# Top-32 attention with a channel mix: groups of four tiles over passes of 256 rows, inverse row sums turned by halves

## The chip, the cores and the metric

The kernel runs on one core of a Trainium2 chip. The metric is device time in microseconds (us), from the first to the last instruction as the runtime measures it; the number compared is the median of several executions. Inside the core five engines work side by side and meet through semaphores: TensorE (PE, matrix products; its weight loads are listed as PEld), VectorE (DVE), ScalarE (ACT), GpSimd (POOL) and SyncE (SP, which here only issues the copies between the chip's main memory and the core).

## The reference

Inputs are q, k, v of shape (8 batches, 8 heads, 576 rows, 64) and the parameters of a channel mix of width 512 with 1024 hidden units.

```python
scores = scale * q @ k.T                       # per batch and head, 576 x 576
kth    = 32nd largest of each row
attn   = exp(where(scores >= kth, scores, -1e9) - rowmax)
attn   = attn / (attn.sum(-1) + 1e-9)
x      = (attn @ v), heads side by side        # (8, 576, 512)
x_prev = x moved down by one row, per batch
xk, xr = mu * x + (1 - mu) * x_prev            # with mu_k and mu_r
k      = relu(xk @ w_k);  v = (k * k) @ w_v
out    = sigmoid(xr @ w_r) * v
```

## The kernel before, in words

**Attention tiles.** Heads go in pairs (HP = 4 pairs). A *tile* is 128 partitions of scores against all 576 keys: in a unit with w > 1 it is 128 query rows of one head (two tiles, j = 0 and 1, for the two heads of the pair); in a unit with w = 1 it is 64 rows of both heads, one head in each half of the partitions. There are 288 tiles. Rows of one batch are cut by PARTS into *visits*, and these into *units* of w = 4, 2 or 1 tiles, since 576 is not a multiple of 256: over four batches there are 14 units for each pair of heads, six of w = 4, four of w = 2, four of w = 1; over the eight batches and four pairs that is 48, 32 and 32 units, 112 in all. A visit loads its queries, its half of the pair's v into one of two buffers, and, on the first visit of a batch and pair, the keys into one of four homes.

**Slots.** The program is written out by hand, slot by slot: slot n starts tile n and carries earlier tiles one stage further, in the sequence ORDER. `score` (L205; L210, or L214 for w = 1) puts the tile into PSUM, ACT copies it out (`keep`, L219), DVE picks candidates over six slots, POOL multiplies (L260), DVE masks (L271). Five slots after the score `turn_tile` (L283) transposes the tile in ten pieces of 64 rows. When the tile is the last of its unit, `inverse` (ACT, L291), `inverse2` (DVE, L295) and `spread` (POOL, L300) make the inverse row sums; one slot later `turn_inverse` (L307, one 128 x 128 transpose for two tiles) and `weigh` (L333, the product with v, 10 matmuls for 128 rows) follow, ACT takes both results out of PSUM (L312 or L316, L339 or L341), and `place` (POOL, L345) multiplies them into x of the batch, in the slot seven after the last score.

**The mix.** The channel mix goes in 18 chunks of 256 rows, each in 40 *pieces* of six or three matmuls (L388 to L390): 8 gate pieces (tile pz), 16 hidden pieces (ph), 16 value pieces (pv). Each chunk runs gates, the second half of the values of the chunk before, hidden, then its own first half of the values. A chunk can begin when all heads have placed its 256 rows; then differences (L358), shares (L363), sums (L368), and a split into a high and a low part (ACT L383, L384) come ahead of its gates. L388 is executed once for each gate or value piece and twice for each hidden piece, 56 times in a chunk.

**The planner.** `Lanes` holds a budget for each engine. PE gets 3.45 a slot, and keeps at most 3.75. A score takes 0.70 from it, a transposed tile 0.45, a unit that is weighed 0.27 w + 0.30 and 0.13 for each transpose of its inverse sums; a piece of the mix takes 0.72, and is issued while at least 0.74 of that is left, at most four a slot:

```python
if done == most or L.free["pe"] < cost * SHARE:
    return done
L.use("pe", cost)
```

In the last 36 slots a piece counts 0.56. After the last tile, VectorE takes over the mix's work of GpSimd.

Of the kernel before, what the change touches and what calls it, by code (L numbers as in the profile page):

```python
# [29 lines left out]
WHOLE = [(0, 4), (256, 4), (512, 1)]  # L30
PARTS = [[(0, 4)], [(256, 4)], [(512, 1)]], [[(0, 1), (64, 2)], [(192, 4)], [(448, 2)]], \
    [[(0, 2)], [(128, 4)], [(384, 2), (512, 1)]], [[(0, 1)], [(64, 4)], [(320, 4)]]
# [15 lines left out]
def topk_attention_channel_mix(ctx: ExitStack, tc: tile.TileContext, q, k, v, mu_k, mu_r, w_k, w_v, w_r, out):  # L48
# [19 lines left out]
    least = consts.tile([128, 3 * B], F32, name="least")  # L68
# [11 lines left out]
    def open_pools(stack, g, sfx):  # L80
# [10 lines left out]
        g.sums = scored[:, :, HS:HS + 128], scored[:, 0, HS + 128:HS + 192]  # L91
# [79 lines left out]

    def load_keys(g, P, batch, hp):
        P.K = g.one.tile([128, 2, HS], F32, name="K", tag=f"K{P.home}")
        for i in range(2):
            nc.sync.dma_start(P.K[i * 64:(i + 1) * 64], heads(k, batch, hp)[:, :, i * HS:(i + 1) * HS].rearrange("h d s -> d h s"))

    def load_queries(g, P, batch, hp, c0, c1):
        P.c0 = c0
        P.qs = g.three.tile([128, 2, c1 - c0], F32, name="qs")
        for i in range(2):  # L180
            nc.sync.dma_start(P.qs[i * 64:(i + 1) * 64], heads(q, batch, hp)[:, :, c0:c1].rearrange("h d s -> d h s"))

    def load_v(g, P, batch, hp):
        P.v = g.two.tile([128, 2, NKC, D], F32, name="v_in")
        P.vr = vr_hf[P.n % 2]
        h = heads(v, batch, hp)
        for j in range(2):
            nc.sync.dma_start(P.v[:, j], h[j, :MAIN].rearrange("(c p) d -> p c d", p=128))
        nc.sync.dma_start(P.vr[64:], h[:, MAIN:].rearrange("h p d -> p h d"))

    def units_of(shape):

        units, tiles = [], []
        for row, w in shape:
            U = Env()
            U.row, U.w = row, w
            units.append(U)
            for k in range(w):
                T = Env()
                T.U, T.k, T.t, T.u, T.j, T.row = U, k, len(tiles), k // 2, k % 2, row + k // 2 * 128  # L200
                T.last = k == w - 1
                tiles.append(T)
        return units, tiles

    def scores(g, P, T):  # L205
        hs = [slice(e * 64, (e + 1) * 64) for e in range(2)]
        x = T.row - P.c0
        if T.U.w > 1:
            for e, h in enumerate(hs):
                nc.tensor.matmul(g.ps[:, e], lhsT=P.qs[h, T.j, x:x + 128], rhs=P.K[h, T.j], start=True, stop=True)  # L210
        else:
            for j in range(2):
                for e, h in enumerate(hs):
                    nc.tensor.matmul(g.ps[hs[j], e], lhsT=P.qs[h, j, x:x + 64], rhs=P.K[h, j], start=True, stop=True)  # L214
        return g.ps
# [57 lines left out]
    def turn_tile(g, T, L):  # L273
        U, j, u = T.U, T.j, T.u
        if T.k == 0:
            U.et = {}
        et = U.et[u, j] = (g.two if j else g.three).tile([128, NKC + 1, 128], F32, name=f"et{j}")
# [11 lines left out]
    def inverse(g, U):  # L289
        rs = U.rs[:, :U.w]  # L290
        nc.scalar.activation(rs, rs, AF.Copy, bias=1e-9)  # L291

    def inverse2(U):
        rs = U.rs[:, :U.w]
        nc.vector.reciprocal(rs, rs)  # L295

    def spread(g, U):
        w, d = U.w, 64 if U.w > 1 else 128
        U.rb = g.one.tile([128, w, d], F32, name="rb")
        nc.gpsimd.tensor_scalar(U.rb, U.rs[:, :w, None].to_broadcast([128, w, d]), 1.0, 1.0, op0=OP.mult, op1=OP.mult)  # L300

    def turn_inverse(g, U, L):
        rb = U.rb.rearrange("p h d -> p (h d)")
        pr = g.pt[:, :, 384:]
        n = (U.w + 1) // 2
        for u in range(n):
            nc.tensor.transpose(pr[:, u], rb[:, u * 128:(u + 1) * 128], ident)  # L307

        def out_():
            U.ri = g.two.tile([128, 256], F32, name="ri")  # L310
            if U.w > 1:
                nc.scalar.activation(U.ri[:, :n * 128].rearrange("p (u q) -> p u q", u=n), pr[:, :n], AF.Copy)  # L312
            else:
                for j in range(2):
                    h = slice(j * 64, (j + 1) * 64)
                    nc.scalar.activation(U.ri[h, :64], pr[h, 0, h], AF.Copy)  # L316
        L.at(0, "late", out_)

    def weigh(g, U, u):
        P = U.P  # L320
        if u == 0:
            U.pa = g.sums[U.w == 1]
        hs = [slice(j * 64, (j + 1) * 64) for j in range(2)]
        if U.w > 1:
            pa = U.pa[:, u]
            ms = [[U.et[u, j][:, c, :] for j in range(2)] for c in range(NKC + 1)]
        else:
            pa = U.pa
            ms = [[U.et[0, 0][:, c, h] for h in hs] for c in range(NKC + 1)]
        for c in range(NKC + 1):  # L330
            for j in range(2):
                lhsT = P.v[:, j, c, :] if c < NKC else P.vr[:, j]
                nc.tensor.matmul(pa[hs[j]], lhsT=lhsT, rhs=ms[c][j], start=(c == 0), stop=(c == NKC))  # L333

    def take_sums(g, U):
        n = U.w // 2
        U.sum = g.two.tile([128, 256], F32, name="sum")
        if n:
            nc.scalar.activation(U.sum[:, :n * 128].rearrange("p (u q) -> p u q", u=n), U.pa[:, :n], AF.Copy)  # L339
        else:  # L340
            nc.scalar.activation(U.sum[:, :64], U.pa, AF.Copy)  # L341

    def place(U):
        n = U.w * 64
        nc.gpsimd.tensor_mul(U.xT[:, U.P.hp, 1 + U.row:1 + U.row + n], U.sum[:, :n], U.ri[:, :n])  # L345

    def begin(g, C, which, i, L):

        X, h0, n, pieces = Env(), 2 * i, C.n, C.pieces
        parts, o = [], 0  # L350
# [259 lines left out]
    def prep(g, P, batch, hp, c0, c1):  # L610
        load_keys(g, P, batch, hp)
        load_queries(g, P, batch, hp, c0, c1)
        load_v(g, P, batch, hp)

# [5 lines left out]
    def pipeline(g):  # L620
# [3 lines left out]
        visits = []  # L624
        for b in range(B):
            for k, shape in enumerate(PARTS[b % 4]):
                visits += [(b, hp, shape) for hp in (range(HP) if k % 2 == 0 else reversed(range(HP)))]
        starts = [0]
        for *_, shape in visits:
            starts.append(starts[-1] + sum(w for _, w in shape))  # L630
        where = [p for p in range(len(visits)) for _ in range(starts[p], starts[p + 1])]
        homes, held = {}, [(-1, None)] * KEYS
        for p, (b, hp, _) in enumerate(visits):
            home = next((h for h, (_, of) in enumerate(held) if of == (b, hp)), None)
            own, free = home is None, 0
            if own:
# [80 lines left out]
        def coming(n):  # L717

            for p in range(1, len(visits)):
                t = n - starts[p]  # L720
                if -8 <= t <= 6:
                    yield Ps[p] if p in Ps else new_pair(p), t
# [258 lines left out]
```

## Time and profile before

| | us |
|---|---|
| median of 3 runs | 1162.88 (1161.68 to 1163.26) |
| the profiled execution | 1162.55 |
| its span, first to last instruction | 1160.7 |
| PE busy | 1094.9 (94%) |
| DVE busy | 1073.9 (93%) |
| ACT busy | 991.4 (85%) |
| POOL busy | 968.3 (83%) |
| mean granted TensorE clock | 0.990 of full speed |

The median is 0.33 us above the profiled execution, which is 1.85 us above its own span. Busy time is a union over the stretch: matmuls are pipelined and their ends are modelled, so a PE that shows no gap can still hold short waits. Times in views are microseconds from the start of the span.

### The profile page before, as it was taken

To read this page: it belongs to the slowest core of one execution; us is meant where nothing else is said; L and a number is where in the kernel's file an instruction comes from. 1 tells how busy PE (TensorE), PEld (TensorE's weight loads), DVE (VectorE), ACT (ScalarE), POOL (GpSimd) and SP (SyncE) were. 2 spreads that over 40 slices of the span, in tenths; PEclk is the share of its full clock that TensorE was granted. 3 is DMA by queue.
4 is the path that set the end of the run, shared out by engine and by line. 5 is a ranking of instruction groups with operands and counts; after the bars stand their busy time and mean duration, and the time that the engine had idled before them with its cause. 6 is when DMAs were issued, how large, how long until landed. Compare 5 with 4: busy or idle time off the path is not lost.

```text
span 1160.7 us, 32775 instructions
## 1 busy us (share of the span) xinstructions
PE 1094.9 (94%) x10625; PEld 854.2 (74%) x10625; DVE 1073.9 (93%) x6009; ACT 991.4 (85%) x2121; POOL 968.3 (83%) x1069
## 2 busy tenths in 40 slices
PE   5777999999999999999999999999999999999998
PEld 2444776768787877787878777787878777878787
DVE  6999999999999999999999999999999999989742
ACT  5889999988898899989898989998989899879631
POOL 5898997998989798989898988898989898979800
PEclk9889999999999999999999999999999999999999
DMA  7434133113331233112211132212331223111100
GB/s 193 124 111 112 30 91 92 49 45 78 77 79 45 64 74 96 49 50 69 70 49 50 29 104 68 69 45 75 80 79 45 62 73 85 44 49 40 30 10 30
DMA packets 161363, 78.77 MB, mean 68 GB/s; under 512 B 125344, under 2 KB 154016, under 8 KB 161184
## 3 DMA queue, kind: packets, MB, share of 16 engines
q1 hardware_dynamic: 161184, 76.59, 25.1%
q8 instruction: 87, 1.43, 0.5%
q14 instruction: 92, 0.75, 0.2%
HBM read 67.11 MB, written 9.44 MB: 66 GB/s over the span
## 4 chain that ended last, share of the span: by engine, by line
PE 51%; POOL 18%; DVE 16%; ACT 12%; issue 2%; DMA 1%; SPq 0%; ACTq 0%; POOLq 0%; DVEq 0%
PE ps L333 10%; PE ps L210 7%; POOL sg L260 6%; PE pt L283 4%; DVE cand L243 4%; PE ph L388 3%; PE pv L388 3%; DVE E L271 3%; PE pv L390 3%; PE ph L389 3%; PE ph L390 3%; DVE seen L843 3%; PE pv L389 3%; PE pz L388 3%; ACT sc L219 3%
## 5 line engine op out<-in xcount | busy, mean ns | idle before, releaser
L243 DVE MAX8 cand<-sc 128x8 f32<-128x82 f32 (+1 forms) x2016 | 467.2, 232 | 10.5 <-ACT sc L219 10.4
L260 POOL TENSOR_TENSOR sg<-sc,sg 128x576 f32<-128x576 f32 x288 | 411.7, 1431 | 48.7 <-ACT sg L257 48.5
L219 ACT ACTIVATE sc<-ps 128x576 f32<-128x576 f32 x288 | 188.0, 653 | 99.6 <-PE ps L210 85.8
L271 DVE SCALAR_TENSOR_TENSOR E<-sc,seen,se 128x576 f32<-128x576 f32 x288 | 232.9, 809 | 0.7 <-DVE cand L243 0.3
L257 ACT ACTIVATE sg<-sc,seen 128x576 f32<-128x576 f32 x288 | 225.7, 784 | 4.4 <-DVE seen L843 3.4
L268 ACT ACTIVATE se<-sc,seen 128x576 f32<-128x576 f32 x288 | 215.7, 749 | 10.4 <-DVE E L271 10.1
L843 DVE MAX8 seen<-sg 128x8 f32<-128x576 f32 x288 | 216.5, 752 | 4.1 <-POOL sg L260 3.7
L210 PE MATMUL ps<-K,qs 64*128 64x288 f32 x1024 | 198.7, 464 | 11.6 <-ACT sc L219 6.3
L286 ACT ACTIVATE et<-pt 128x640 f32<-128x640 f32 x288 | 204.3, 710 | 6.0 <-PE pt L283 4.0
L283 PEld LDWEIGHTS pt<-ident,E 64*128 64x128 f32 x2880 | 132.9, 139 | 75.2 <-ACT sg L257 17.5
L246 DVE MAX8 seen<-cand 128x8 f32<-128x56 f32 x864 | 177.4, 205 | 0.1
L388 PE MATMUL ph<-xh,wk 128*128 128x256 f32 x576 | 172.2, 299 | 0.0
L333 PE MATMUL ps<-et,v_in 128*64 128x128 f32 (+1 forms) x2560 | 162.0, 269 | 8.4 <-ACT sc L219 7.2
L389 PE MATMUL ph<-xl,wk 128*128 128x256 f32 x576 | 162.2, 282 | 0.0
L390 PE MATMUL ph<-xh,wk 128*128 128x256 f32 x576 | 162.0, 281 | 0.0
L333 PEld LDWEIGHTS ps<-et,v_in 128*64 128x64 f32 x2560 | 131.4, 138 | 39.6 <-ACT sc L219 13.1
L283 PE MATMUL pt<-ident,E 64*128 64x64 f32 x2880 | 140.3, 224 | 15.3 <-DVE E L271 9.0
L210 PEld LDWEIGHTS ps<-K,qs 64*128 64x128 f32 x1024 | 79.5, 189 | 74.0 <-issue 24.7
L388 PE MATMUL pv<-wv,hh 128*128 128x512 f32 x288 | 123.7, 429 | 0.0
L390 PE MATMUL pv<-wv,hl 128*128 128x512 f32 x288 | 114.3, 397 | 8.7 <-POOL hl L409 8.7
L249 DVE MATCH_REPLACE8 cand<-seen,cand 128x56 f32<-128x56 f32 x576 | 115.4, 200 | 0.0
L389 PE MATMUL pv<-wv,hh 128*128 128x512 f32 x288 | 113.5, 394 | 0.0
(103 smaller groups left out, 2234.5 us busy)
## 6 DMA issues: line engine op xcount, KB each, us to landing
v_in<-in_v SPq DMA_DIRECT2D x192, 128.0 KB, 2.6
qs<-in_q SPq DMA_DIRECT2D x96, 128.0 KB, 2.9
K<-in_k SPq DMA_DIRECT2D x64, 144.0 KB, 3.0
out<-eb SPq DMA_DIRECT2D x36, 256.0 KB, 2.5
vr_in<-in_v SPq DMA_DIRECT2D x96, 32.0 KB, 2.5
hh<-in_moe_w_v SPq DMA_DIRECT2D x6, 512.0 KB, 4.1
qs<-in_q SPq DMA_DIRECT2D x32, 96.0 KB, 2.6
hh<-in_moe_w_k SPq DMA_DIRECT2D x5, 512.0 KB, 4.2
```

What stands on the lines that cost most here:

```text
L210: nc.tensor.matmul(g.ps[:, e], lhsT=P.qs[h, T.j, x:x + 128], rhs=P.K[h, T.j], start=True, stop=True)
L219: nc.scalar.activation(T.sc.rearrange("p (e k) -> p e k", e=2), T.ps, AF.Copy)
L243: nc.vector.max(T.cand[:, 8 * i:8 * i + 8], T.sc[:, CUTS[i]:CUTS[i + 1]])
L257: nc.scalar.activation(T.side, T.sc, AF.Sign, bias=T.top[:, 23:24], scale=-1.0, accum_out=T.cnt)
L260: nc.gpsimd.tensor_mul(T.side, T.sc, T.side)
L271: nc.vector.scalar_tensor_tensor(T.e, T.sc, T.thr, g.pe, op0=OP.is_ge, op1=OP.mult, accum_out=T.rs)
L283: nc.tensor.transpose(g.pt[:, n, c * 64:(c + 1) * 64], T.e[h, k0:k0 + 128], ident[h, h])
L333: nc.tensor.matmul(pa[hs[j]], lhsT=lhsT, rhs=ms[c][j], start=(c == 0), stop=(c == NKC))
L388: nc.tensor.matmul(ps, lhsT=sh, rhs=mh, start=first, stop=False)
L389: nc.tensor.matmul(ps, lhsT=sh, rhs=ml, start=False, stop=False)
L390: nc.tensor.matmul(ps, lhsT=sl, rhs=mh, start=False, stop=last)
L843: nc.vector.max(M.top[:, 24:32], M.side)
```

## The change

The rows of all batches are now one sequence of 4608, cut into 18 passes of 256 rows. In each pass and pair of heads there is one *group* of four tiles, always weighed at once; 72 groups in all. A pass that crosses from one batch to the next (64 + 192, 128 + 128 or 192 + 64 rows; six of the 18) has two parts: keys, queries and v are loaded for both. Where the seam lies inside a block of 128 rows (16 of the 144 blocks), its two tiles hold 64 rows of each batch: each is scored in four matmuls, and the block is weighed in 20 matmuls of 64 columns and not 10 of 128. The other tiles of w = 1 are gone. There are still 288 tiles, 288 slots, and 96 parts (before, 96 visits).

The inverse sums of a group are turned by four transposes of 64 rows each, in the form that `turn_tile` uses, and no longer by 128 x 128 transposes. The planner charges a weighed group 1.38, as before for w = 4, and its transposes 0.16 where w = 4 had 0.26. The homes of the keys are chosen by which is needed again last; in a pass over a seam two batches' keys are live for each pair, so some are loaded again. By the rule in the diff it is four more loads of a pair's keys for each such pass, so 56 in place of 32, each of two copies. v is loaded when the second user before in the same order of parts has been weighed. The copy of a batch's last rows (`rest`, L649) is only made when it is needed. `least` has 18 columns for 24.

```diff
-PARTS = [[(0, 4)], [(256, 4)], [(512, 1)]], [[(0, 1), (64, 2)], [(192, 4)], [(448, 2)]], \
-    [[(0, 2)], [(128, 4)], [(384, 2), (512, 1)]], [[(0, 1)], [(64, 4)], [(320, 4)]]
+BLOCK = 64
+ROWS = 4 * BLOCK
...
+    def load_queries(g, P):
+        P.qs = g.three.tile([128, 2, ROWS], F32, name="qs")
+        for Q in P.parts:
+            for i in range(2):
+                nc.sync.dma_start(P.qs[i * 64:(i + 1) * 64, :, Q.c0:Q.c0 + Q.m], heads(q, Q.batch, P.hp)[:, :, Q.row:Q.row + Q.m].rearrange("h d s -> d h s"))
...
     def scores(g, P, T):
+        x, (Q, R) = T.u * 128, P.blocks[T.u]
+        if Q is R:
             for e, h in enumerate(hs):
+                nc.tensor.matmul(g.ps[:, e], lhsT=P.qs[h, T.j, x:x + 128], rhs=Q.K[h, T.j], start=True, stop=True)
         else:
+            for i, N in enumerate((Q, R)):
                 for e, h in enumerate(hs):
+                    nc.tensor.matmul(g.ps[hs[i], e], lhsT=P.qs[h, T.j, x + i * 64:x + (i + 1) * 64], rhs=N.K[h, T.j], start=True, stop=True)
...
+    def turn_inverse(g, P, L):
+        rb = P.rb.rearrange("p (u h) d -> p u (h d)", u=2)
         pr = g.pt[:, :, 384:]
-        n = (U.w + 1) // 2
-        for u in range(n):
-            nc.tensor.transpose(pr[:, u], rb[:, u * 128:(u + 1) * 128], ident)
+        for u in range(2):
+            for n, h in enumerate(hs):
+                nc.tensor.transpose(pr[:, n, u * 64:(u + 1) * 64], rb[h, u], ident[h, h])
...
+    def weigh(g, P, u):
+        Q, R = P.blocks[u]
+        for q, N in [(slice(0, 128), Q)] if Q is R else zip(hs, (Q, R)):
+            for c in range(NKC + 1):
                 for j in range(2):
+                    lhsT = N.v[:, j, c, :] if c < NKC else N.vr[:, j]
+                    nc.tensor.matmul(g.sums[hs[j], u, q], lhsT=lhsT, rhs=P.et[u, j][:, c, q], start=(c == 0), stop=(c == NKC))
...
+    def place(P, Q):
+        rows, cols = slice(1 + Q.row, 1 + Q.row + Q.m), slice(Q.c0, Q.c0 + Q.m)
+        nc.gpsimd.tensor_mul(Q.xT[:, P.hp, rows], P.sum[:, cols], P.ri[:, cols])
...
+        keys, held, loads_ = {}, [(-1, None)] * KEYS, 0
+        for n, (p, hp, parts) in enumerate(groups):
+            for b, *_ in parts:
+                home = next((h for h, (_, of) in enumerate(held) if of == (b, hp)), None)
+                if home is None:
+                    ahead = [next((m for m in range(n, len(groups)) if of and groups[m][1] == of[1] and any(x[0] == of[0] for x in groups[m][2])), len(groups)) for _, of in held]
+                    home = max((h for h in range(KEYS) if held[h][0] < max(n - 1, 0) and ahead[h] > n), key=lambda h: (ahead[h], -held[h][0]))
+                    keys[n, b] = home, max(4 * n - (5 if n > 1 else 4), 4 * held[home][0] + 4)
+                held[home] = n, (b, hp)
+        vs, users = {}, []
+        for n, (p, hp, parts) in enumerate(groups):
+            for b, *_ in parts:
+                vs[n, b] = len(users) % 2, max(4 * n - 2, 4 * users[-2] + 10 if len(users) > 1 else 0)
+                users.append(n)
...
                 if last:
-                    L.use("pe", 0.27 * W.U.w + 0.30)
+                    L.use("pe", 1.38)
...
-                    L.use("pe", 0.13 * ((W.U.w + 1) // 2))
+                    turn_inverse(g, W.P, L)
+                    L.use("pe", 0.16)
```

## Rows read from the trace of the kernel before

**Rows 1.** Busy time by stretch: length, then each engine, granted clock, DMA

```profile
260.30:436.50 176.20, 173.95 (x1758) 137.43 (x1754) 170.37 (x990) 157.97 (x346) 157.70 (x176) 1.00 0.27 70
436.50:666.60 230.10, 228.77 (x2282) 184.16 (x2280) 226.93 (x1315) 210.02 (x440) 205.95 (x215) 1.00 0.22 57
666.60:944.90 278.30, 273.06 (x2814) 216.13 (x2814) 270.93 (x1571) 251.79 (x555) 246.73 (x279) 1.00 0.27 70
944.90:1113.70 168.80, 163.97 (x1599) 133.34 (x1596) 141.09 (x779) 135.89 (x291) 136.95 (x151) 0.99 0.18 47
1113.70:1160.70 47.00, 39.66 (x221) 34.03 (x219) 18.23 (x33) 9.50 (x16) 0.02 (x1) 0.97 0.07 25
```

**Rows 2.** The same stretches, L219 alone (one for each tile): ACT busy (count)

```profile
260.30:436.50 176.20, 31.41 (x48) 1.00 0.27 70
436.50:666.60 230.10, 41.78 (x64) 1.00 0.22 57
666.60:944.90 278.30, 49.61 (x76) 1.00 0.27 70
```

**Rows 3.** The same stretches, L388 alone: PE busy (count), PEld busy (count)

```profile
260.30:436.50 176.20, 59.23 (x166) 32.00 (x166) 1.00 0.27 70
436.50:666.60 230.10, 79.47 (x222) 41.98 (x222) 1.00 0.22 57
666.60:944.90 278.30, 91.39 (x256) 49.44 (x256) 1.00 0.27 70
```

**Rows 4.** The chain of waits in order of time: start, length, what

```profile
427.60 1.24 PE ps L333 x20
428.84 0.64 PE ps L214 x8
429.48 0.45 PE pt L283 x10
429.94 0.26 PE pt L307
430.19 0.24 PE pz L388
...
431.59 0.73 PE ps L333 x20
...
433.43 0.43 PE pz L388
...
511.61 0.37 PE pt L307 x2
512.69 2.33 PE ps L333 x40
```

**Rows 5.** Groups of instructions by line and shape: VectorE's reciprocal

```profile
L295 DVE RECIPROCAL rs<-rs 128x4 f32<-128x4 f32 x48 | 7.7, 161 | 2.9 <-ACT rs L291 2.9
```

**Rows 6.** Timeline behind the last placement

```profile
1112.97 0.74 POOL L345 TENSOR_TENSOR xT<-sum,ri 128x256 f32<-128x256 f32 x1 [10.80 <-ACT sum L339]
...
1115.29 1.19 ACT L383 ACTIVATE xh<-xm 128x512 fp32r<-128x512 f32 x2
...
1119.30 1.29 DVE L384 TENSOR_TENSOR xl<-xm,xh 128x512 fp32r<-128x512 f32 x2
...
1121.51 0.39 PE L388 MATMUL pz<-wr,xh 128*128 128x512 f32 x1
```

**Rows 7.** DMA issues: count, KB each, median us to landing

```profile
K<-in_k SPq DMA_DIRECT2D x64, 144.0 KB, 3.0
...
qs<-in_q SPq DMA_DIRECT2D x32, 32.0 KB, 2.2
```

**Rows 8.** Timeline of PE at a late wait and eight matmuls later

```profile
1020.85 0.59 PE L390 MATMUL pv<-wv,hl 128*128 128x512 f32 x1 [1.82 <-POOL hl L409]
...
1024.22 0.54 PE L389 MATMUL pz<-wr,xh 128*128 128x512 f32 x1
```

**Rows 9.** Busy time and granted clock just after it

```profile
1022.00:1023.00 1.00, 1.00 (x4) 0.72 (x3) 0.24 (x1) 0.00 (x0) 1.00 (x3) 0.50 0.00 0
```

More of the change, by code (lines that the diff above doesn't have):

```diff
@@ L183, in load_v, with __init__ @@
[L183 to L186, printed above, removed]
-        for j in range(2):
[L188 to L203, printed above, removed]
+    class Part:
+        def __init__(self, b, row, c0, m, batch):
+            self.b, self.row, self.c0, self.m, self.batch = b, row, c0, m, batch
@@ new lines, in load_v, with open_group @@
+    def load_v(g, Q, hp, which):
+        Q.v = g.two.tile([128, 2, NKC, D], F32, name="v_in")
+        Q.vr = vr_hf[which]
+        h = heads(v, Q.batch, hp)
+        for j in range(2):
+            nc.sync.dma_start(Q.v[:, j], h[j, :MAIN].rearrange("(c p) d -> p c d", p=128))
+        nc.sync.dma_start(Q.vr[64:], h[:, MAIN:].rearrange("h p d -> p h d"))
+    def open_group(P):
+        of = [Q for Q in P.parts for _ in range(Q.m // BLOCK)]
+        P.blocks = [of[2 * u:2 * u + 2] for u in range(2)]
+        P.tiles, P.et = [], {}
+        for t in range(4):
+            T = Env()
+            T.P, T.t, T.u, T.j = P, t, t // 2, t % 2
+            T.last = t == 3
+            P.tiles.append(T)
@@ L273, in turn_tile @@
     def turn_tile(g, T, L):
[L274 to L277, printed above, removed]
+        j, u = T.j, T.u
+        et = T.P.et[u, j] = (g.two if j else g.three).tile([128, NKC + 1, 128], F32, name=f"et{j}")
         g.pt = g.psT.tile([128, 2, 512], F32, name="pt")
@@ L287, in turn_tile, with inverse @@
         L.at(*EVAC, out_)
[L289 to L303, printed above, removed]
+    def inverse(g, P):
+        nc.scalar.activation(P.rs, P.rs, AF.Copy, bias=1e-9)
@@ L309, in out_ @@
         def out_():
[L310 to L313, printed above, removed]
-                for j in range(2):
[L315 to L345, printed above, removed]
+            P.ri = g.two.tile([128, 256], F32, name="ri")
@@ L622, in pipeline @@
         g.by = nc.gpsimd
[L624 to L636, printed above, removed]
-                home = held.index(min(held, key=lambda x: x[0]))
-                free = starts[held[home][0] + 1] - 1
-            held[home] = p, (b, hp)
-            homes[p] = own, home, free
@@ L641, in pipeline @@
-        xT, tiles, state = {}, {}, {"heads": [0] * HP, "wait": 0, "start": 0, "held": []}
+        groups = []
+        for p in range(B * S // ROWS):
+            parts, o = [], p * ROWS
+            while o < (p + 1) * ROWS:
+                b, row = divmod(o, S)
+                m = min(S - row, (p + 1) * ROWS - o)
+                parts.append((b, row, o - p * ROWS, m))
+                o += m
+            groups += [(p, hp, parts) for hp in (range(HP) if p % 2 == 0 else reversed(range(HP)))]
@@ L643, in save @@
+        vs, users = {}, []
[3 more added lines that the diff above has]
+                users.append(n)
+        xT, tiles, state = {}, {}, {"heads": [0] * HP, "wait": 0, "start": 0, "held": [], "K": {}}
         def save(size=CH):
@@ L656, in chunks @@
                 C = Env()
-                C.n, C.rows, C.pieces = size, out_rows[t0:t0 + size], None
+                C.n, C.rows, C.pieces, C.first, C.begun = size, out_rows[t0:t0 + size], None, t0 // S, 0
+                state["chunk"] = C
                 def have(i, C=C, t0=t0, size=size):
@@ L950, in topk_attention_channel_mix @@
                 C.n = min(CH, S - t0)
[L951 removed]
+                C.rows, C.pieces, C.have, C.begun = rows[t0:t0 + C.n], [(xT, t0, C.n)], lambda i: True, 0
                 parts.append(C)
```

209 lines of the change are left out of this document (105 added, 104 removed).

## The prediction, before the changed kernel was run

> **What bounds the kernel now.** I read the page first: PE is busy for 94% of the span, DVE for 93%, ACT and POOL for 85 and 83%. No engine stands out, so the question goes to the stages. The view of busy time by stretch gives them [rows 1]; I cut it at multiples of 16 tiles. From 260 to 945 us PE and DVE are both at 97 to 99%: a slot there is as long as the longer of the two. From 945 to 1114 us, where the planner counts a piece of the mix at 0.56, PE has 97% and DVE 84%. From 1114 us to the end only the mix is left, and PE with it.
>
> Then I counted. The copy of the scores (L219) is executed once for a tile [rows 2], and L388 56 times in the 40 pieces of a chunk [rows 3], so a piece is 1.4 of L388. The stretch from 436.5 to 666.6 us is the 64 tiles in which nearly every unit has w = 4: 230.1/64 = 3.595 us a slot, and 222/64/1.4 = 2.48 pieces in it. The stretch ahead of it mixes units of 4, 2 and 1: 176.2/48 = 3.671 us and 166/48/1.4 = 2.47 pieces. The one behind it mixes them too: 278.3/76 = 3.662 us and 256/76/1.4 = 2.41 pieces. So slots with narrow units are longer and carry less of the mix. PE's gaps in the pure stretch are 1.3 us of 230.1; in the two mixed ones 2.3 of 176.2 and 5.2 of 278.3 [rows 1].
>
> The planner explains the pieces, and this is arithmetic from the code. A slot that weighs w = 4 has 3.75 - 0.70 - 0.45 - 1.64 = 0.96 left, one piece; the next three have 2.6 or a little less, three pieces each. That is 10 in four slots, 40 in the 16 slots in which the tiles of a chunk are made: the mix keeps its distance. With w = 1 each slot has 3.75 - 1.15 - 0.70 = 1.90, two pieces, and 0.46 is left, under the 0.53 that a third needs: 8 in four slots. The mix falls back by half a piece in each of those 32 slots, 16 pieces in all, and has to make them up at the end.
>
> **The change part by part.**
>
> *Weighing.* The chain of waits has the three bursts: 2.33 us for w = 4, 1.24 for w = 2, 0.73 for w = 1 [rows 4]. Before: 48 x 2.33 + 32 x 1.24 + 32 x 0.73 = 174.9 us. After: 72 x 2.33 = 167.8, and something for the 16 blocks with a seam. Their twenty matmuls of 64 columns have the columns of a plain block, so nothing is the lower bound; two bursts of w = 1 (1.46 for 2.33 - 1.24 = 1.09) are the upper one, 16 x 0.37 = 5.9 us. A burst has an entry of 1.24 - 1.09 = 0.15, which the seam pays once, so I take 2 x (0.73 - 0.15) - 1.09 = 0.07 each, 1.1 us. PE is spared 174.9 - 168.9 = 6.0 us, between 1.2 and 7.1.
>
> *Inverse sums.* A first gate behind a turned tile takes 0.43 us, behind one transpose of L307 0.24; one such transpose takes 0.26, two take 0.37 [rows 4]. So 0.19 is a change-over that is paid in one place or the other, and the transposes cost 0.07 and 0.18: 48 x 0.18 + 64 x 0.07 = 13.1 us. After, they have exactly the form of L283, ten in 0.45 us, so 72 x 4 x 0.045 = 13.0 us. I count nothing, with 2 us either way.
>
> *Scores of seam blocks.* 32 tiles in four matmuls, as there were 32 tiles of w = 1 (0.64 us, L214 [rows 4]). Nothing, but they now fall into stretches whose pace I take from pure slots; that comes below.
>
> *Small work of a unit.* 112 become 72 of each of the inverse's addition, reciprocal, spread, and the two copies out of PSUM. On DVE a reciprocal is 161 ns [rows 5], narrower ones hardly less, so 40 x 0.16 = 6.4 us go. ACT and POOL are spared more but have slack of 8 to 12% in the mixed stretches [rows 1]. I count these at nothing by themselves: PE's pace covers them. Were PE not there, DVE's 6.4 us would be the floor of the gain; the pure stretch, with DVE at 98.6%, shows that its pace is near the DVE's floor too, so I go no lower than that pace.
>
> *Copies.* Queries and v go in as many copies as before; the keys in 24 x 2 more, each 3.0 us to landing [rows 7], at least four slots (14.4 us) ahead of their first score. v of a seam group has both buffers live, so the next group's v is issued behind one weighing and needed at the next, four slots later; six copies and one landing fit in that. I count nothing; the rival below says when that fails. Some query pieces are 64 rows wide; the old ones of 32 KB landed in 2.2 us [rows 7], sooner than any other. The Trainium skill, in DMA: Bandwidth & Descriptors, Specifications, asks for at least 512 B a descriptor for line rate, and a run of 64 rows is 256 B; by the rows such a piece still lands in 2.2 us, so the trace gives no sign of harm here.
>
> **The sum**, against the profiled execution's 1162.55 us:
>
> 1. Mixed stretches. 124 slots at 3.595 us are 445.8 us, for 176.2 + 278.3 = 454.5: 8.7 us less, with (222/64 x 124 - 166 - 256)/1.4 = 6 pieces more in them. Three of the four passes with a seam inside a block fall here, 24 tiles, each a four-matmul score plus change-over that I put at 0.1 us (an estimate from 0.64 and 0.07 above, bounds 0 and 0.15). I take 6 us; bounds 1 and 8.7. The lower bound stands for waits that stay although their units go.
> 2. Before 260 us the weights are being made. Half a piece in 8 narrow slots is 4 pieces; I count no time, bounds 3 either way.
> 3. So some 10 pieces reach the last two stretches done. A value or gate piece is three matmuls at 0.24 [rows 4], 0.7 us; 7 us of PE's work leave 215.8 us. How much shows depends on the end. The last placement ends at 1113.7 us; the first gate that needs it starts at 1121.5, behind the split, ACT at 1115.3 and DVE at 1119.3 [rows 6]. PE is covered meanwhile by value pieces. With the mix further on, the cover is gone and the gates wait for the chain itself: 1.6 us to ACT's split, 1.19 and 1.29 for its two halves [rows 6], 4.1, with the meetings between them about 5 us for 7.8. A second split stands between gates and hidden pieces; 8 value pieces, 5.6 us, cover it now, and by the same two lengths 2.5 us of it would be left. So the last stretch can give 2.8 + 3.1 at most; I take 3. The stretch from 945 to 1114 us gives the rest, 4.
>
> 6 + 0 + 4 + 3 = 13 us: 1149.6 us for the execution, and with the median 0.33 above it **1150 us**.
>
> **Rivals.**
>
> *The waits stay* (0.20). Only PE's own 6.0 us go; the mix, further on, meets its data sooner and starves. For it: in the last stretch each of two splits would leave PE idle for 2.5 to 5 us, and an idle PE has shown its price: a wait of 1.82 us [rows 8], and behind it a granted clock of 0.50, the lower level of 1.2 GHz [rows 9]. The eight matmuls behind that wait start (1024.22 - 1020.85)/8 = 0.42 us apart, where 0.24 is usual: about 1.5 us lost each time. Against it: PE's gaps in the mixed stretches are real and the pure stretch lacks them. 6.0 - 1.5 + 1 = about 5.5 us, so 1157. The Trainium skill, in TensorE: Matmul & The Clock Gate, HAM oscillation, says that idle gaps in PE's work bring it to half its clock again and again; rows 8 and 9 agree, and by that rule this rival is the one to watch.
>
> *More goes* (0.10). Term 1 in full, 8.7, all 7 of term 3, and 5 of the last stretch: 20.7 us, 1142.
>
> *No change* (0.08). The end hangs on the last placement, and the gain before it is given back as waiting. This needs the slots not to get shorter, the mixed stretches being held by POOL's chain; 1163.
>
> *Slower: loads of seam groups come late* (0.09). SP works in order, and v waits there for a weighing; keys and queries stand behind it. Were each of the 24 seam groups to hold its first score by 1 us (a third of a landing), 24 - 13 = 11 us more, 1174; it decides from 13/24 = 0.54 us a group. Against it: DMA is 22 to 27% busy in these stretches [rows 1] and the lead is four slots.
>
> **How the numbers follow.** My forecast has 0.53; its own range is 1145 to 1155. Two tenths of a per cent, 2.3 us, is about what a measurement of this kernel can tell from no change. Faster: 0.53 + 0.20 + 0.10 = 0.83; same 0.08; slower 0.09. For 8 in 10 the range leaves out the slower case, most of no change and a little below the larger gain: 1141 to 1160.
>
> **What would show it.** L219 at about 3.60 us a slot and L388 at 3.47 a slot from 260 us on, in every stretch; weighing bursts of 2.33 us, 72 of them, 16 a little longer; transposes of the inverse at 0.045 each; 112 copies of keys, and no score waiting for a DMA; at the last placement fewer than 56 pieces left, and gates about 5 us behind it. Wrong would be: slots over 3.65 us with DVE or POOL ending the waits; a score that waits for keys or queries; or a last stretch of 47 us again, with PE idle and a clock of 0.50 in it.

## The result and the profile after

The changed kernel takes 1171.85 us (median of 4 runs, 1171.16 to 1172.81), the kernel before 1162.73 beside it: a ratio of 1.0081, interval 1.0065 to 1.0097. It is slower by 0.8%, where I forecast 1.1% faster. The profiled execution took 1172.81 us, with a span of 1171.0.

The page of the changed kernel: busy time by engine, and the chain that ended last.

```profile
PE 1094.3 (93%) x10753; PEld 851.7 (73%) x10753; DVE 1073.5 (92%) x5957; ACT 968.4 (83%) x1969; POOL 961.5 (82%) x1013
PE 42%; POOL 28%; DVE 19%; ACT 6%; issue 3%; SPq 1%; DMA 0%; ACTq 0%; POOLq 0%
```

TensorE and VectorE are as busy as before; what changed is who ends the waits. GpSimd had 18% of the chain before and has 28% now.

The busy time of the changed kernel by stretch, cut at the same tiles as [rows 1] (slots 64, 112, 176, 252) and at the end of the last placement; columns as there. Under it the matmuls of L370, the L388 of before, in the second and third stretch (PE busy and count, PEld busy and count), as [rows 3].

```profile
265.80:442.40 176.60, 172.85 (x1777) 136.59 (x1776) 170.69 (x981) 155.12 (x319) 155.42 (x165) 1.00 0.31 79
442.40:677.40 235.00, 230.01 (x2317) 184.01 (x2318) 227.54 (x1308) 206.75 (x425) 206.11 (x210) 1.00 0.23 61
677.40:957.80 280.40, 273.67 (x2862) 216.58 (x2862) 270.37 (x1554) 245.40 (x505) 247.87 (x264) 1.00 0.31 79
957.80:1129.91 172.11, 164.61 (x1612) 133.78 (x1608) 140.90 (x772) 129.87 (x264) 132.69 (x138) 0.96 0.18 47
1129.91:1171.00 41.09, 32.00 (x183) 26.86 (x181) 15.04 (x28) 8.30 (x14) 0.00 (x0) 0.97 0.06 23
...
442.40:677.40 235.00, 80.35 (x225) 42.00 (x225) 1.00 0.23 61
677.40:957.80 280.40, 95.82 (x270) 50.39 (x270) 1.00 0.31 79
```

Set against [rows 1], with the terms of the prediction:

| stretch | forecast | before | after | difference |
|---|---|---|---|---|
| start to slot 64 | 0 | 260.3 | 265.8 | +5.5 |
| slots 64 to 252 | -6 | 684.6 | 692.0 | +7.4 |
| slot 252 to the last placement | -4 | 168.8 | 172.1 | +3.3 |
| last placement to the end | -3 | 47.0 | 41.1 | -5.9 |

The pace is now one throughout: 176.6/48, 235.0/64 and 280.4/76 us are 3.68, 3.67 and 3.69 us a slot. I expected one pace too, but the 3.595 of the plain stretch. That stretch itself, where the groups had four tiles already, went from 230.1 to 235.0 us; the sum had no term for it. So of the +7.4 us in slots 64 to 252, 4.9 fall in the plain stretch and 2.5 in the 124 mixed slots (457.0 us for 454.5), for which 6 less were forecast. L370 is executed 225/64 = 3.52 and 270/76 = 3.55 times a slot, as many as the forecast's 3.47 and a little more: the pieces came, the time did not go.

The waits of the changed kernel in its slots 112 to 176 (engine, tile and line, what was waited for: us in total, times, longest).

```profile
PE pv L372 <- POOL hl L391: 4.3, 4, 1.1
...
PEld pv L372 <- POOL hl L391: 6.0, 4, 1.5
```

Sixty-four slots are four passes of 16, and in each of them one value matmul waits for the fine part `hl` that GpSimd makes of the hidden activations. The view of waits of the kernel before shows no such line for its plain stretch, but one for each of its mixed stretches (260.3 to 436.5 us, then 666.6 to 944.9):

```profile
PE pv L390 <- POOL hl L409: 2.1, 3, 1.4
...
PE pv L390 <- POOL hl L409: 2.2, 3, 1.0
```

So part of what made the mixed stretches slow may be this same wait, and not the narrow units; no run parts the two. One of the four on TensorE's timeline (start, length, [idle before, releaser]), and GpSimd up to it:

```profile
541.44 0.40 PE L371 MATMUL pv<-wv,hh 128*128 128x512 f32 x1
542.89 0.50 PE L372 MATMUL pv<-wv,hl 128*128 128x512 f32 x1 [1.05 <-POOL hl L391]
...
535.87 2.52 POOL L366 TENSOR_TENSOR xl<-xm,xh 128x512 fp32r<-128x512 f32 x2
538.35 1.44 POOL L263 TENSOR_TENSOR sg<-sc,sg 128x576 f32<-128x576 f32 x1
539.74 0.75 POOL L326 TENSOR_TENSOR xT<-sum,ri 128x256 f32<-128x256 f32 x1
540.43 1.05 POOL L390 TENSOR_TENSOR r<-r 128x512 f32<-128x512 f32 x1
541.56 1.27 POOL L391 TENSOR_TENSOR hl<-r,hh 128x512 fp32r<-128x512 f32 x1
```

GpSimd runs without a gap through all of these rows. The pair's square `hh` is there at 539.73 (ACT's L389), but GpSimd first has a mask (L263) and a placement (L326) in hand, and `hl` comes at 542.83. The third matmul starts 542.89 - 541.44 = 1.45 us after the second, where 0.23 is usual: 1.22 us a pass, 4.9 us in 64 slots. That is as much as 235.0 - 230.1, but the two need not be equal: hold1 below has longer waits of this kind and a shorter stretch.

Late in the kernel something else happens. TensorE's timeline, and then a view of busy time in steps of 2 us (length, PE, PEld, DVE, ACT, POOL, granted clock, DMA):

```profile
1017.37 0.40 PE L372 MATMUL pv<-wv,hl 128*128 128x512 f32 x1
1017.70 0.76 PE L213 MATMUL ps<-K,qs 64*128 64x288 f32 x4
...
1020.20 0.82 PE L213 MATMUL ps<-K,qs 64*128 64x288 f32 x4 [1.43 <-ACT sc L222]
...
1022.85 1.33 PE L213 MATMUL ps<-K,qs 64*128 64x288 f32 x4 [0.56 <-ACT sc L222]
...
1025.85 0.79 PE L370 MATMUL pz<-wr,xh 128*128 128x512 f32 x1
1026.44 0.63 PE L371 MATMUL pz<-wr,xh 128*128 128x512 f32 x1
1026.86 0.63 PE L372 MATMUL pz<-wr,xl 128*128 128x512 f32 x1
1027.29 0.63 PE L370 MATMUL pz<-wr,xh 128*128 128x512 f32 x1
...
1017.00:1019.00 2.00, 1.78 (x17) 0.98 (x16) 1.64 (x10) 2.00 (x6) 0.73 (x1) 1.00 0.71 155
1019.00:1021.00 2.00, 0.80 (x4) 0.37 (x4) 2.00 (x10) 2.00 (x4) 1.41 (x1) 1.00 0.49 152
1021.00:1023.00 2.00, 0.98 (x13) 0.79 (x12) 2.00 (x16) 2.00 (x6) 1.41 (x1) 0.63 0.26 97
1023.00:1025.00 2.00, 1.27 (x6) 0.48 (x8) 2.00 (x11) 2.00 (x5) 1.23 (x2) 0.50 0.00 0
1025.00:1027.00 2.00, 2.00 (x17) 1.69 (x18) 2.00 (x14) 2.00 (x6) 2.00 (x3) 0.50 0.01 4
1027.00:1029.00 2.00, 2.00 (x13) 1.29 (x13) 2.00 (x13) 1.75 (x4) 1.96 (x3) 0.66 0.02 4
```

Between 1017.8 and 1025.8 us there is no piece of the mix at all. The pieces of one chunk are used up, and the gates of the next stand behind the chain that makes their input. It begins with a placement at 1001.38 us; ACT's split and GpSimd's fine part, its end, come when the gap is already there (ACT's and GpSimd's timeline):

```profile
1023.27 1.16 ACT L365 ACTIVATE xh<-xm 128x512 fp32r<-128x512 f32 x2
...
1024.14 2.52 POOL L366 TENSOR_TENSOR xl<-xm,xh 128x512 fp32r<-128x512 f32 x2
```

TensorE is half idle meanwhile, and the granted clock falls to its lower level, 1.2 GHz. From the second on, the matmuls of the gates that follow start 0.42 to 0.43 us apart instead of 0.23. A second pause comes later in the same 36 slots, 10 us without a piece, and the granted clock is 0.50 from 1077 to 1079 us; what it waited for stays open:

```profile
1070.47 0.39 PE L372 MATMUL pv<-wv,hl 128*128 128x512 f32 x1
...
1080.81 0.50 PE L370 MATMUL pv<-wv,hh 128*128 128x512 f32 x1
```

At the end the forecast held in kind, and the gain was larger: 5.9 us where I took 3. The last placement ends at 1129.91 us; the first gate behind it starts 3.7 us later, where I expected about 5, and the hidden pieces wait 1.20 us for their split:

```profile
1133.64 0.39 PE L370 MATMUL pz<-wr,xh 128*128 128x512 f32 x1
...
1141.79 0.38 PE L370 MATMUL ph<-xh,wk 128*128 128x256 f32 x1 [1.20 <-ACT xh L365]
```

### The profile page after: what moved, and what is told of

The parts are those of the page before. It is cut to its first block, busy times and chain, and to the rows that moved or that the text cites. A ratio compares the mean times of both kernels' runs of the same rounds, so it can differ in the third digit from the quotient of the medians.

```text
span 1171.0 us, 32806 instructions
## 1 busy us (share of the span) xinstructions
PE 1094.3 (93%) x10753; PEld 851.7 (73%) x10753; DVE 1073.5 (92%) x5957; ACT 968.4 (83%) x1969; POOL 961.5 (82%) x1013
## 4 chain that ended last, share of the span: by engine, by line
PE 42%; POOL 28%; DVE 19%; ACT 6%; issue 3%; SPq 1%; DMA 0%; ACTq 0%; POOLq 0%
POOL sg L263 9%; PE ps L318 8%; PE ps L213 6%; POOL hl L391 5%; DVE cand L246 4%; DVE E L274 4%; POOL r L390 3%; PE ph L370 3%; PE pv L370 3%; PE pt L284 3%; DVE seen L827 3%; POOL xl L366 3%; PE pv L372 3%; PE ph L371 3%; PE ph L372 3%
## 5 line engine op out<-in xcount | busy, mean ns | idle before, releaser
L263 POOL TENSOR_TENSOR sg<-sc,sg 128x576 f32<-128x576 f32 x288 | 410.5, 1428 | 60.4 <-ACT sg L260 58.5
L271 ACT ACTIVATE se<-sc,seen 128x576 f32<-128x576 f32 x288 | 217.0, 754 | 8.5 <-DVE E L274 7.7
L370 PE MATMUL ph<-xh,wk 128*128 128x256 f32 x576 | 171.5, 298 | 1.2 <-ACT xh L365 1.2
L318 PEld LDWEIGHTS ps<-et,v_in 128*64 128x64 f32 x2560 | 136.0, 141 | 26.3 <-issue 16.0
L370 PE MATMUL pv<-wv,hh 128*128 128x512 f32 x288 | 125.1, 434 | 0.0
L370 PEld LDWEIGHTS ph<-xh,wk 128*128 128x128 f32 x576 | 108.4, 188 | 8.9 <-ACT xh L365 1.6
```

Of the source, the lines that this page charges most:

```text
L263: nc.gpsimd.tensor_mul(T.side, T.sc, T.side)
L271: nc.scalar.activation(g.pe, T.sc, AF.Exp, bias=T.nb, scale=SCALE)
L318: nc.tensor.matmul(g.sums[hs[j], u, q], lhsT=lhsT, rhs=P.et[u, j][:, c, q], start=(c == 0), stop=(c == NKC))
L370: nc.tensor.matmul(ps, lhsT=sh, rhs=mh, start=first, stop=False)
```

## The experiments

Two theories at first. *Place*: the mix now stands at one constant distance behind the tiles (the first gate of a chunk comes 12 slots after the chunk's last tile, counted by the starts of the score copies; 15 in the plain stretch of before, 13 to 18 in the mixed ones), and at that distance the hidden pair's fine part falls behind other work of GpSimd. *Parts*: a new operation costs more than I booked, the half transposes or the seam groups' early loads.

### Moving the mix, turning by whole tiles, loading later, a calmer end

hold3:

```
-                work(MOST)
+                if not 64 <= n < 67:
+                    work(MOST)
```

> The changed kernel, with no piece of the mix issued in slots 64 to 66, so that the mix stands about three slots further behind the tiles from there on (gates of a chunk start 15 slots after its last tile, as in the pure stretch of before, and not 12). Theory A (the pace hangs on how far the mix stands behind): the slots from 112 to 176 fall from 235.0 us for 64 to about 231, and TensorE's waits for the fine part of the hidden values (hl) get fewer. Theory B (the form of the inverse transposes or the loads of the groups set the pace): the 64 slots stay at 235 us within 1 us. For the end A expects the mix not to run out of rows near 1017 us, so that the stretch from slot 252 to 287 takes about 140 us and not 148.

full_turn (four half transposes become two of 128x128, the copy behind them likewise):

```
-            for n, h in enumerate(hs):
-                nc.tensor.transpose(pr[:, n, u * 64:(u + 1) * 64], rb[h, u], ident[h, h])
+            nc.tensor.transpose(pr[:, u], rb[:, u], ident)
```

> The changed kernel, with the inverse sums of a group turned by two transposes of 128 x 128 as before. Theory A: within 2 us of the changed kernel (1171.85), 64 slots from 112 at 235 us within 1 us. Theory B: near 1165 and 231 us.

v_late (`4 * n + 2 if n == 1 else 4 * n - 2` for `4 * n - 2` in the slot of the values' load):

> The changed kernel, with v of the second group issued in slot 6, as before, and not in slot 2. The start of slot 32 is at 148.7 us in the changed kernel and 143.6 before. If the early v pushes back the copies of weights behind it, slot 32 starts at about 144 and the whole takes about 5 us less; if the start differs for another cause (the half transposes, the granted clock), slot 32 stays at 147 to 150 us.

no_haste (`HASTE` 0.72 for 0.56):

> The changed kernel, with a piece of the mix counted at 0.72 in the last 36 slots too, and not 0.56. In the changed kernel the mix catches up, finds no placed rows near 1017 us and TensorE stands idle, with a lower granted clock behind it; slots 252 to 287 take 148.0 us, the rest 65.3. If that starving is what the end costs: slots 252 to 287 near 129 us (35 at 3.69), the rest longer by the 15 or so pieces not done, 11 us, in sum some 8 us less. If the starving costs nothing, the sum of 213 us stays within 2 us or grows.

Measured on one chip, beside 1163.56 of the kernel before: hold3 1158.28 us, ratio 0.9964 (0.9949 to 0.9979); full_turn 1170.92, 1.0061 (1.0047 to 1.0076); v_late 1169.18, 1.0044 (1.0015 to 1.0073); no_haste 1164.56, 1.0015 (1.0003 to 1.0027).

Three slots without a piece of the mix turn the loss into a gain. Slots 112 to 176 take 229.3 us in hold3, the lines that wait for `hl` are gone there, and GpSimd does the last pair's work ahead of the placement. The waits of hold3 in that stretch, and GpSimd at the same point of a pass as above:

```profile
PE ps L318 <- ACT sc L222: 1.4, 4, 0.4
...
541.72 1.42 POOL L263 TENSOR_TENSOR sg<-sc,sg 128x576 f32<-128x576 f32 x1
543.09 1.05 POOL L390 TENSOR_TENSOR r<-r 128x512 f32<-128x512 f32 x1
544.22 1.28 POOL L391 TENSOR_TENSOR hl<-r,hh 128x512 fp32r<-128x512 f32 x1
...
546.83 0.75 POOL L326 TENSOR_TENSOR xT<-sum,ri 128x256 f32<-128x256 f32 x1
```

At the end hold3 gains little: slots 252 to 287 take 141.1 us for 143.8, and 8.8 us without a piece of the mix come at 1059.7 us. full_turn has 234.8 us in slots 112 to 176: the half transposes are not the cause. v_late has slot 32 at 143.8 us, as expected if the early load pushes the weights back; but full_turn, which loads early, has it at 143.7, so this does not show the load's price. no_haste has 235.0 us in slots 112 to 176, but slots 252 to 287 take 129.3 us for 143.8, and what follows 77.9 for 69.4: 207.2 for 213.2 in all, 6.0 us less.

### What the place is: other distances, and less work on GpSimd

hold1 and hold4 are hold3 with one and four slots in the place of three. skip_sq books GpSimd's `r*r` as before and leaves it out:

```
-        q = L.soft("pool", 1.17, lambda: g.by.tensor_mul(X.r[:, :, :n], X.r[:, :, :n], X.r[:, :, :n]), h, rank=1)
+        q = L.soft("pool", 1.17, lambda: None, h, rank=1)
```

> The changed kernel, with no piece of the mix in slot 64 alone, so that the mix stands about one slot further back from there. Theory A says that the pace of 235.0 us for slots 112 to 176 hangs on one wait a pass: a value piece that waits for GpSimd to write the fine part (hl) of the last hidden values, 6.0 us in four passes; with three slots of delay it was gone and the 64 slots took 229.3 us. With one slot of delay A expects some of it to be left or moved: between 230 and 235 us, and where hl still ends TensorE's waits the loss against 229 us is about the sum of these waits. A rival (any delay frees the slots, since fewer pieces are issued in all) expects 229 us at once.

> As with three slots, but four (64 to 67): the mix stands about 16 slots behind. Theory A: no wait for hl, so 229 to 231 us for slots 112 to 176, and the end later than with three slots by the pieces not yet done, up to 2 us. The rival that the pace follows the distance itself, the further the better, expects below 229 us.

> The changed kernel without the multiplication r * r on GpSimd (its place in the plan is kept, so the sequence of all other instructions is the same; the fine part is then made from r and not from its square). It ends about 1.05 us sooner before each fine part. Theory A: the wait of 1.5 us for hl in each pass falls to 0.5 or nothing, and the 64 slots from 112 take 229 to 231.5 us with the mix as close as in the changed kernel. The rival that the closeness itself (the pieces in the slots) sets the pace expects 234 to 235 us.

Single runs: 1168.85, 1180.12 and 1145.7 us. hold1 takes 233.8 us in slots 112 to 176, inside its range, and its waits for `hl` there are longer than the 4.3 us of the changed kernel:

```profile
PE pv L372 <- POOL hl L391: 5.2, 4, 1.4
```

skip_sq shows that the loss goes through GpSimd: with 1.04 us less of GpSimd's work on each pair and the pieces in the same slots as in the changed kernel, slots 112 to 176 take 227.6 us and nothing on TensorE waits for GpSimd there. That is less than expected, and less than hold3's 229.3: 16 multiplications are gone from these slots, 16.65 us of GpSimd's time, and only four of them stand directly ahead of a late `hl`. So the run speaks for GpSimd's load as a whole, and does not single out the one wait. hold4 missed its expectation by far: 236.1 us at a distance of 16. More distance is not better. Its waits in slots 112 to 176, and GpSimd ahead of the longest kind:

```profile
PE pt L305 <- POOL rb L298: 4.2, 4, 1.4
PE pv L372 <- POOL hl L391: 2.0, 4, 0.5
...
547.23 1.29 POOL L391 TENSOR_TENSOR hl<-r,hh 128x512 fp32r<-128x512 f32 x1
548.49 1.40 POOL L263 TENSOR_TENSOR sg<-sc,sg 128x576 f32<-128x576 f32 x1
549.87 0.40 POOL L298 TENSOR_SCALAR rb<-rs 128x256 f32<-128x256 f32 x1
```

Here the pair's work stands ahead of a mask and of the group's spread `rb`, and the inverse transposes come late as well.

### Is it the distance, and does it act on the kernel before too?

before_hold1 is the kernel before with no piece in slot 112.

> The kernel before with no piece of the mix in slot 112, where its first stretch of plain groups begins, so that the mix stands one slot further behind the tiles there (16 instead of 15). Theory A (the pace hangs on how the mix stands to the tiles in a pass, through the wait for GpSimd's fine part, and not on the shape of the groups): slots 112 to 176, 230.1 us in the kernel before, take about the 236 that hold4 took at a distance of 16. Rival (plain groups run at 230 whatever the distance): 230 within 1.

It took 231.3 us there (1163.25 in all, a single run): a miss. The same distance of 16 costs the kernel before 1.2 us and the changed one 6.8. The plan books the turn of a group at 0.26 us in one and 0.16 in the other, so hold4_cost and before_hold1_cost exchange the two prices, `L.use("pe", 0.26)` for 0.16 and 0.08 for 0.13 a transpose. hold7 and hold2 hold the mix for seven and for two slots.

> The kernel hold4 with the four half transposes booked in the plan at 0.26 us, as the kernel before books the two of a group, instead of 0.16; the instructions are the same, only the places of the mix's pieces move. Theory P (what slows slots 112 to 176 is the place of single pieces in a pass, which the plan's costs set, so that hold4 and before_hold1 differ at the same distance of 16): about the 231 of before_hold1. Rival (the half transposes themselves are slow at this distance, since they wait for GpSimd's spread): 236, as hold4.

> The kernel before_hold1 with the plan's cost of a transpose of inverse sums 0.08 instead of 0.13 us, so that a group of four is booked at 0.16 as in the changed kernel; the instructions are the same. Theory P: slots 112 to 176 take about the 236 of hold4 instead of 231.3. Rival: 231.3 within 1.

> The changed kernel with no piece of the mix in slots 64 to 70: a distance of 19. If only the place of the pieces within a group of four slots counts (19 and 15 have the same), slots 112 to 176 take about the 229.3 of hold3. If every slot of distance costs, as 15 to 16 did, over 236.

> The changed kernel with no piece in slots 64 and 65: a distance of 14, the one place in a group of four slots that no run has shown (12 and 16: 235.0 and 236.1, 13: 233.8, 15: 229.3). If the pace changes step by step with the place, between 229.3 and 233.8; if 15 is the only one where the value pieces come behind GpSimd's fine part, 233 to 236.

The booked price is not it: 236.1 and 231.3 us, as before the exchange (1173.48 and 1172.21 in all; the second is 9 us longer than before_hold1, 8.5 of them behind slot 252, and why stays open). hold7 took 229.6 us at a distance of 19 (1158.25 in all), as its expectation has it if the place within a group of four slots counts; hold2 came to rest at 15 by itself, and took 229.3 (1162.16), so no run shows the distance of 14. I then counted, from the starts of pieces between the starts of the score copies, in which slot of a group's four the pass's last hidden matmul stands (0 is the slot of the group's first score):

| kernel | slots behind | last hidden in | slots 112 to 176, us |
|---|---|---|---|
| changed kernel, full_turn | 12 | 0 | 235.0, 234.8 |
| hold1 | 13 | 1 | 233.8 |
| hold4, hold4_cost | 16 | 0 | 236.1 |
| hold3, hold2 | 15 | 3 | 229.3 |
| hold7 | 19 | 3 | 229.6 |
| before | 15 | 3 | 230.1 |
| before_hold1, before_hold1_cost | 16 | 3 | 231.3 |

So the pace goes with the slot of the group in which the hidden pieces end, and not with the distance as such; before_hold1 is no exception to that: there the last of them comes one piece earlier than in hold4. I found this order in the runs afterwards, and no run placed the hidden pieces alone. In the runs of the changed kernel this slot is the remainder of the distance divided by four, so before_hold1 alone tells the slot and the remainder apart. That the place acts through GpSimd is shown by skip_sq. Why the two plans differ by that one piece at the same distance stays open.

### The end

before_calm is the kernel before with `HASTE` 0.72.

> The kernel before with one number changed: the pieces of the last 36 slots are placed at the cost 0.72 instead of 0.56, as in no_haste. Theory A (in the last slots the mix catches up with its tiles, runs out of placed rows, TensorE stands idle and its granted clock falls; this hits both kernels): the stretch from slot 252 to the end, 215.7 us in the kernel before, falls to about the 208 of no_haste, and the kernel takes 1155 to 1158 us. Rival (the kernel before has no such gap, since its mix stands more slots behind the tiles at slot 252): no gain, 1163, or a loss of a few us, because more pieces are left for the last stretch.

1157.97 us, ratio 0.9956 (0.9940 to 0.9972): the time is as theory A has it. From slot 252 to the end 210.6 us are left of 215.7. So the cheap last slots are a fault that the kernel before has as well, but not for the reason of theory A: its mix never pauses for more than 5.3 us in slots 252 to 287, where the changed kernel's pauses are 8.5 and 10.3 us. What TensorE waits for most there is the fine part again, 2.8 us, and the fall of the clock comes behind the longer of the two waits [rows 8, 9]; in before_calm 0.7 us of it are left (view of waits, before, slots 252 to 287):

```profile
PE pv L390 <- POOL hl L409: 2.8, 2, 1.8
```

The fault weighs a little more in the changed kernel, 6.0 us of no_haste against 5.1 here. The distance at which the mix comes to the last slots (12 in the changed kernel, 18 before) does not explain that: hold3, at 15, loses most, as the next runs show.

### Put together

best is the changed kernel with hold3, v_late and no_haste; best_full turns by whole tiles as well; best_early loads the values as early as the changed kernel.

> Three edits to the changed kernel together: no piece in slots 64 to 66, a piece counted at 0.72 to the end, v of the second group in slot 6. From hold3 (1158.28), the 2.7 us of the late v and, for the end, the 207.2 us that the calm end took behind slot 252 with the mix three slots closer, plus 5.3 us for the 7.5 pieces that are left: 212.5 in place of 217.1. That gives 1158.28 - 2.7 - 4.6 = about 1151 us. If the gains at the end overlap with those of the delay, 1155.

> The kernel best with the inverse sums of a group turned by two transposes of 128x128 instead of four of 64 rows. If the half transposes cost or save nothing: 1144, within 1.5 us of best. If they save what the prediction bounded at most, 2 us more than best.

> The kernel best with the values' load of the second group ahead of the weights in the queue again, as in the changed kernel. If the early load costs what v_late showed against the changed kernel: 1146.7, with slot 32 some 2 us later than in best. Rival (the 2.7 us were the start's own spread from chip to chip): 1144, within 1.5 us of best.

best 1144.02 us, ratio 0.9832 (0.9816 to 0.9848): 7 us less than I expected. The difference lies behind slot 252, where 204.5 us took the place of the 212.5 expected; hold3 took 217.0 there, so the calm end gives 12.5 us once the mix stands in the better place. On another chip best_full 1146.23, 0.9851 (0.9826 to 0.9876), and best_early 1146.47, 0.9857 (0.9832 to 0.9881). These two differ by the load of the values as well as by the transposes, and best_full is 2.2 us above best on another chip, so the totals do not settle the price of the half transposes. Slots 64 to 287 do better: 803.1 us in best_full, 801.6 to 802.2 in the four profiles of best and best_early (two of them from the next section). The half transposes save about 1 us there; in the changed kernel, slots 64 to 252, they cost 0.3 (692.0 against 691.7 of full_turn). best_early and before_calm ran on one chip and differ, beside the three held slots, by the change alone: 1146.47 against 1157.97 us. best_early by stretch (slots 64, 112, 176, 252, 287):

```profile
263.60:436.10 172.50, 168.51 (x1755) 135.04 (x1755) 169.82 (x981) 154.21 (x318) 152.44 (x163) 0.99 0.32 81
436.10:665.40 229.30, 227.90 (x2322) 184.53 (x2318) 226.46 (x1309) 207.40 (x425) 205.85 (x210) 1.00 0.24 63
665.40:939.10 273.70, 272.26 (x2870) 217.97 (x2866) 269.10 (x1554) 245.98 (x503) 245.62 (x260) 1.00 0.32 81
939.10:1065.70 126.60, 125.42 (x1319) 100.82 (x1315) 124.03 (x717) 113.66 (x233) 113.99 (x121) 1.00 0.23 57
1065.70:1143.90 78.20, 70.12 (x502) 60.19 (x498) 33.57 (x91) 26.26 (x49) 16.70 (x18) 0.98 0.06 22
```

A slot takes 3.58 to 3.62 us from 64 to 287. Against before_calm that is 261.3 to 263.6 up to slot 64, 684.2 to 675.5 up to 252, 126.7 to 126.6 up to 287, and 83.9 to 78.2 behind it: +2.3, -8.7, -0.1 and -5.7, together 12.2 us.

### The start

late_pair and early_pair are best and best_early once more, side by side.

> The kernel best once more, on the same chip as best_early. If the values' early load costs at the start: 2 to 3 us below early_pair. Rival (v_late against the changed kernel, and best against best_early, differed by their chips and by the spread of the start): within 1 us of early_pair.

> The kernel best_early once more, on the same chip as best: with an early load that costs, 2 to 3 us above late_pair, and no run of it below the median of late_pair; without, within 1 us.

1146.14 us (1144.95 to 1146.72) and 1147.35 (1146.83 to 1148.47): 1.2 us, between the two expectations, with no run of the early load below the late one's median. The early load costs about 1 us by this, with four runs of each and intervals that overlap (0.9837 to 0.9870 and 0.9847 to 0.9880), and not the 2.7 by which v_late was ahead of the changed kernel on another chip.

## Why the prediction was wrong

**The step that failed is term 1.** It took the 3.595 us of the plain stretch as the price of a slot with a group of four, and laid it on all 124 mixed slots. It is the price of such a slot with the mix in a good place. In the mixed stretches of before TensorE waited for the fine part too, 2.1 and 2.2 us, so their longer slots may not be the narrow units' doing alone. The prediction even had the reason in hand: "That is 10 in four slots, 40 in the 16 slots [...]: the mix keeps its distance." It does; the same pieces fall into the same slots of every pass. But then the distance at which it settles decides on every pass, and I never asked which one that would be. In the mixed stretches of before the distance moves between 13 and 18 slots; after the change it stood at 12 slots from slot 64 to 252, in a place that costs (235.0 - 229.3)/4 = 1.4 us a pass. That is 692.0 - 675.7 = 16.3 us against hold3 over these 188 slots. In a good place the term comes out inside its bounds: best_early takes 446.2 us for the 124 mixed slots, before_calm 454.1, so 7.9 less where 6 were taken and 8.7 were the most; the plain stretch gives another 0.8. What the prediction named as a sign of being wrong, slots over 3.65 us with GpSimd ending the waits, is what came; GpSimd's chain as the limit stood only in the rival *No change*, with 0.08, and it cost more than that rival allowed.

**Term 2** had 0 with 3 us either way; the profiled execution gives +5.5. The kernels with the change reach slot 64 at 261.1 to 267.8 us (16 executions), those without at 260.3 to 261.6 (4). Part of it may be the clock: counted in steps of 1 us from 30 to 262 us, the granted clock is at its lower level for 17 to 24 us in the four, 20 to 31 in the sixteen, 27 in the changed kernel. But hold2 and late_pair have the same 31 us and reach slot 64 at 267.8 and 263.1 us, so the clock does not account for it alone. The early values' load is about 1 us. What sets the rest, and why it differs between executions, stays open.

**Term 3** was right in sum for a calm end (-5.8 us of best_early against before_calm, -7 forecast) and wrong in its first part for the changed kernel: slot 252 to the last placement became 3.3 us longer. The prediction saw that a mix further on loses its cover, but looked for it behind the last placement alone. There the last stretch gave 5.9 us, all that the text held possible. The planner's cheap last 36 slots use the same cover up earlier: the gap at 1018 us. "The waits stay" names this price [rows 8, 9]. The Trainium skill, in TensorE: Matmul & The Clock Gate, HAM oscillation, says that idle gaps in TensorE's work bring its clock down again and again. The steps from 1019 to 1029 us agree.

**Small terms.** Inverse transposes nothing, with 2 us either way: right, by the stretches of full_turn and best_full. The seam blocks' weighing: the forecast was 0.07 us each, and the chain has the burst of a seam group at 2.41 us where the others take 2.33, so 0.08. The chain of the changed kernel has a weighing at 2.33 us and the four half transposes at 0.12 us up to the next instruction, where I had 0.18 for four:

```profile
1012.53 0.12 PE pt L305 x4
...
1013.55 2.33 PE ps L318 x40
```

**Loads of seam groups late**, the rival whose 1174 us is close to the result, is not what happened. In the whole run scores wait for one load only, the first queries, and the stretches with seams inside a block are no longer than slots 112 to 176, which have none (3.68 and 3.69 us a slot against 3.67). The group of the scores' matmuls, with what ended the idle time before them:

```profile
L213 PE MATMUL ps<-K,qs 64*128 64x288 f32 x1024 | 200.3, 467 | 15.8 <-ACT sc L222 10.6 <-DMA qs<-in_q 5.2
```

What would have warned me: GpSimd was 90% busy in the plain stretch [rows 1], 205.95 us of 230.1, and the slack that I counted it at nothing for is an average over many slots. A value piece that needs two of GpSimd's operations in a row, behind a mask and a placement, meets the busy slots, not the average.

## What to carry to other kernels

When two streams of work share in-order engines and a change makes their pattern regular, ask at which offset it locks, and follow one pass at that offset through the busiest helper engine; a pace read from another stretch holds only for the offset of that stretch. Try the offset by itself, by holding one stream back for a few slots: three slots were worth 13.6 us here (1171.85 to 1158.28, on two chips; 16.3 in slots 64 to 252). Look at a planner's end game whenever one stream gets further ahead, since it takes from the same cover.

## What the runs showed of the hardware

After the gap in the mix the granted clock was 0.63, 0.50, 0.50 and 0.66 in the steps from 1021 to 1029 us, the last two with TensorE fully busy: what follows a gap pays too, here 7 to 11 us after it began. And giving TensorE more work at the end lost time: booking a piece at 0.56 instead of 0.72, which places more of them in a slot, cost 5.1 us from slot 252 to the end in the kernel before, 6.0 in the changed one and 12.5 in hold3. Else the engines' work took as long as before: a weighing of four tiles 2.33 us in both kernels (2.41 at a seam), a tile's transposes 0.22 us each in both, and GpSimd's mask 1.43 us in both.
